# A banded attention and feed-forward kernel: its list scheduler models the SBUF port pair, one integer step works on halfwords, and the matrix engine is given unread products

## The chip, the cores and the metric

The kernel runs on one core of a Trainium2 chip. The metric is device time in microseconds of one execution. The engines are named as in the profile: PE (matrix engine), PEld (its weight loads), DVE (vector), ACT (scalar), POOL (GpSimd) and SP (the queue that issues most transfers).

## The reference, cut to what matters

```python
scores = scale * np.matmul(q, k.transpose(0, 1, 3, 2))        # q, k, v: 4 x 8 heads x 768 x 64
keep = is_global | is_local                                    # first 8 columns, or the last 96
scores = np.where(keep, scores - slopes * dist, -1000000000.0)
a = softmax(scores)
x = matmul(a, v)            # then laid out as 4 x 768 x 512
xn = (x - mu) / np.sqrt(var + 1e-06) * g_ln
ch = np.maximum(xn @ w_ch1, 0.0) @ w_ch2                       # 512 -> 2048 -> 512, float64 weights
out = x + ch
```

## The kernel before, in words

The 3072 rows are 24 tiles of 128. A tile *t* goes through attention over two blocks of keys (its own and the one before it; the first tile of each of the four batches has one block and is called short). Two tiles make a chunk *c* for the feed-forward part. The four short tiles come first (t = 0 to 3, chunks 0 and 1) and are computed in float32 straight from the loaded data; the other tiles use pairs of float16 numbers, a high part and a low part, and so do all feed-forward products (three products for each one wanted).

Before the feed-forward part can start, the float64 weights have to become such pairs. `weight(n)` (line 279) does it for 16 pieces, 8 of the first matrix and 8 of the second. A piece is loaded (`wb`), and then goes through six passes of 1024 elements per partition: `below` (`wr`, ACT), `signs` (`ws`, DVE, copies the sign bit into the low word), `sizes` (`wz`, ACT), `whole` (`ww`, DVE), `upper` (`wu`, the high part: POOL for the pieces in LIGHT, else ACT) and `lower` (`wl`, the low part by a subtraction, POOL).

The names of the other steps, which are also keys of the plan: for a short tile `tk`, `tq` are transpositions of keys and queries on PE, `km`, `qm` the copies out of PSUM. For group *g* of a tile: `S` scores (PE), `R` mask and minimum (DVE), `E` exponentials (ACT), then for short tiles a transposition `tp` (PE) and its copy `pl`; for the other tiles `ph` (the high part, DVE), `pl` (the low part, POOL) and `pt` (a transposing transfer); `P` is the product with the values (PE, tile `pv`). Then `X` divides, `B`, `A`, `W`, `C` normalize (`W` is a power of 128 x 1 numbers on POOL), `xr`, `xt`, `xh`, `xl` transpose the result into `xT`. `F{c}_{f}` is a step of the first feed-forward product (24 matmuls, 256 columns wide, needs both tiles' `xl` and pieces 2j and 2j+1 of the weights, j = f // 4), followed by `hh` (ACT) and `hl` (DVE); `G` is a step of the second product.

The order on every engine is not that of the code: `class Plan` (line 78) takes all steps as tasks with an engine, a cost, predecessors, a rank and buffer tokens, runs a list scheduler over them with those costs, and the instructions of each engine are written in the order that comes out. Nothing is reordered on the chip afterwards, so a task whose input is late holds up what is queued behind it on its engine. Each PSUM and SBUF buffer pool is a token count in `plan.room`. Before, the plan takes an engine as given for each task, and each engine as independent of the others:

```python
LIGHT = (0, 1, 2, 3, 4, 5, 9, 11, 13, 14)
task(f"ws{n}", "DVE", 1.22, signs, [f"wr{n}"], rank=rank)
task(f"ww{n}", "DVE", 1.22, whole, [f"wz{n}"], rank=rank)
task(f"wl{n}", "POOL", 2.4, lower, [f"wu{n}"], rank=rank)
```

All instructions that the plan writes carry line 169 in the profile (the body of `made` in `Lane`), so rows are told apart by their tiles: `w2h`, `w2l`, `st` are the places where weight pieces are worked on, `f` the PSUM tile of a feed-forward step, `r` the reciprocal of the exponentials' sum at the start of `X`.

## Time and profile before

| | us |
|---|---|
| median of 3 runs (645.90 to 646.12) | 646.03 |
| the profiled execution | 646.06 |
| its span, first to last instruction | 644.30 |
| outside the span | 1.76 |
| PE busy | 608.2 |
| DVE busy | 398.3 |
| ACT busy | 277.3 |
| POOL busy | 218.2 |

[...] A start-to-start distance of two neighbours in an engine's timeline is what an instruction costs in a full queue; its duration is a little longer, since neighbours overlap.

### The profile page before, as it was taken

To read this page: it belongs to the slowest core of one execution; us is meant where nothing else is said; L and a number is where in the kernel's file an instruction comes from. 1 tells how busy PE (TensorE), PEld (TensorE's weight loads), DVE (VectorE), ACT (ScalarE), POOL (GpSimd) and SP (SyncE) were. 2 spreads that over 40 slices of the span, in tenths; PEclk is the share of its full clock that TensorE was granted. 3 is DMA by queue.
4 is the path that set the end of the run, shared out by engine and by line. 5 is a ranking of instruction groups with operands and counts; after the bars stand their busy time and mean duration, and the time that the engine had idled before them with its cause. 6 is when DMAs were issued, how large, how long until landed. Compare 5 with 4: busy or idle time off the path is not lost.

```text
span 644.3 us, 13414 instructions
## 1 busy us (share of the span) xinstructions
PE 608.2 (94%) x5266; PEld 436.3 (68%) x5266; DVE 398.3 (62%) x953; ACT 277.3 (43%) x729; POOL 218.2 (34%) x172
## 2 busy tenths in 40 slices
PE   5678699799999999999999999999999999999995
PEld 4567488455885885885885875875875875874852
DVE  4799999896575565546555646555645645546740
ACT  3877477554363353344443343443443433330200
POOL 4476667574243223223223222322323222120000
PEclk9857799999999999999999999999999999999999
DMA  8941777968996665688577585686686664241000
GB/s 240 308 187 66 213 180 201 244 130 164 221 162 137 153 132 108 139 159 156 129 146 139 114 160 113 152 172 115 143 144 117 121 125 82 51 66 34 17 4 35
DMA packets 247303, 88.26 MB, mean 137 GB/s; under 512 B 237376, under 2 KB 237376, under 8 KB 247232
## 3 DMA queue, kind: packets, MB, share of 16 engines
q1 hardware_dynamic: 246944, 87.32, 62.0%
q8 instruction: 43, 0.70, 0.5%
q14 instruction: 28, 0.23, 0.1%
q10 hardware_dynamic: 288, 0.00, 0.0%
HBM read 38.01 MB, written 6.29 MB: 69 GB/s over the span
## 4 chain that ended last, share of the span: by engine, by line
PE 83%; DVE 9%; ACT 3%; issue 2%; DMA 1%; POOL 1%; ACTq 0%; DVEq 0%; POOLq 0%
PE f L169 71%; PE s L169 6%; PE pv L169 5%; DVE st L169 3%; DVE w2h L169 1%; ACT T L169 1%; DVE h L169 1%; DMA nn<-in_n_local_dram 1%; DVE w2l L169 1%; ACT w2h L169 1%; DVE T L169 1%; DMA pT<-pn 0%; DVE qn L169 0%; POOL w1l L169 0%; ACT st L169 0%
## 5 line engine op out<-in xcount | busy, mean ns | idle before, releaser
L169 PE MATMUL f<-xT,w1h 128*128 128x256 f16 x1536 | 260.6, 276 | 8.3 <-DVE h L169 8.3
L169 PE MATMUL f<-w2h,h 128*128 128x512 f16 x768 | 238.2, 379 | 3.7 <-DVE h L169 3.7
L169 PE MATMUL f<-xT,w1l 128*128 128x256 f16 x768 | 212.2, 276 | 0.1
L169 PEld LDWEIGHTS <-h 128*128 128x128 f16 x1152 | 109.7, 98 | 126.2 <-issue 2.3
L169 POOL TENSOR_TENSOR pn<-T,pn 128x512 f16<-128x512 f32 x80 | 95.4, 1193 | 232.9 <-DVE pn L169 121.4
L169 PEld LDWEIGHTS <-w1h 128*128 128x128 f16 x1536 | 150.3, 99 | 27.4 <-DVE h L169 6.0
L169 PE MATMUL f<-w2l,h 128*128 128x512 f16 x384 | 145.5, 379 | 0.0
L169 ACT ACTIVATE h<-f 128x512 f16<-128x512 f32 x96 | 56.7, 591 | 93.1 <-PE f L169 92.8
L169 ACT ACTIVATE T<-T,mn 128x256 f32<-128x256 f32 (+1 forms) x192 | 92.4, 482 | 4.3 <-ACT mn L169 0.4
L169 DVE SCALAR_TENSOR_TENSOR h<-f,h 128x512 f16<-128x512 f32 x96 | 65.5, 686 | 31.2 <-ACT h L169 30.7
L169 PEld LDWEIGHTS <-w1l 128*128 128x128 f16 x768 | 76.2, 99 | 10.1 <-POOL w1l L169 0.4
L169 DVE CAST pn<-T 128x512 f16<-128x512 f32 x80 | 38.2, 479 | 67.7 <-ACT T L169 66.0
L169 DVE CUSTOM_DVE_ANT_0 T<-s,mask 128x256 f32<-128x256 f32 (+1 forms) x192 | 68.0, 395 | 13.4 <-PE s L169 13.1
L169 ACT ACTIVATE mn<-nm 128x2 f32<-128x2 f32 (+1 forms) x88 | 17.6, 200 | 136.2 <-DVE nm L169 136.1
L169 PE MATMUL s<-kT,qT 128*128 128x128 f16 (+1 forms) x704 | 58.9, 233 | 2.8 <-DVE d L169 2.8
L169 PEld LDWEIGHTS <-pT 128*128 128x128 f16 x960 | 38.9, 98 | 12.4 <-DMA pT<-pn 0.6
L169 POOL TENSOR_TENSOR kn<-kf,kn 128x512 f16<-128x512 f32 x24 | 29.0, 1209 | 45.6 <-ACT kn L169 36.4
L169 DVE SCALAR_TENSOR_TENSOR x<-f,x 128x512 f32<-128x512 f32 x24 | 16.2, 687 | 45.6 <-PE f L169 45.6
L169 PE MATMUL pv<-vn,pT 128*128 128x64 f16 x960 | 41.0, 193 | 0.1
L169 PEld LDWEIGHTS <-qT 128*128 128x128 f16 x640 | 38.5, 98 | 2.4
L169 POOL TENSOR_TENSOR rs<-rs,half 128x1 f32<-128x1 f32 x24 | 23.6, 983 | 48.9 <-DVE rs L169 47.8
L169 ACT ACTIVATION_READ_ACCUMULATOR T<-T,mn 128x1 f32 x192 | 35.8, 186 | 0.0
(114 smaller groups left out, 498.6 us busy)
## 6 DMA issues: line engine op xcount, KB each, us to landing
st<-in_moe_w_ch_dram SPq DMA_DIRECT2D x10, 1024.0 KB, 5.8
kf<-in_k_dram SPq DMA_DIRECT2D x28, 256.0 KB, 3.9
vf<-in_v_dram SPq DMA_DIRECT2D x28, 256.0 KB, 3.4
qf<-in_q_dram SPq DMA_DIRECT2D x24, 256.0 KB, 4.0
out_dram<-x SPq DMA_DIRECT2D x24, 256.0 KB, 2.5
qT<-qT SPq DMA_DIRECT2D x40, 128.0 KB, 2.5
w2h<-in_moe_w_ch_dram SPq DMA_DIRECT2D x3, 1024.0 KB, 8.7
w2l<-in_moe_w_ch_dram SPq DMA_DIRECT2D x3, 1024.0 KB, 7.0
```

The source lines that it names most:

```text
L169: ins = getattr(self.engine, name)(*args, **kw)
```

## The change

- The plan knows that DVE and POOL exclude each other: a task with `port=True` on DVE, and every task on POOL, starts no earlier than the last such task ended (`port` in `order`).
- A task may name several engines with a cost on each. The plan then takes the engine on which it would end first, with ACT favoured by 1.1 us and POOL burdened by 1.1 us (`SIDE`). This holds for both mask tables, the copies out of PSUM, the high and low parts of keys, values, queries and probabilities, `wu`, `wl`, `xr` and `hh`. LIGHT is gone.
- `signs` writes the top halfword of the low word from the top halfword of the high word (one source, 16 bits), where it combined two 32-bit operands.
- `blank` is a product of the identity with itself, 512 columns wide, into a PSUM bank that nobody reads. Where the plan sees PE idle before time 90, it writes as many of them as fit the gap at 0.22 us each.
- The bank for them is taken from `pv`, which has one bank left where it had two.
- The numbers that set ranks (QUICK, PIECE, START) and many costs are new.

```diff
-QUICK = (0.0, 2.2, 22.1, 36.5)
-PIECE = (20.2, 5.8, 11.5)
-START = 43.0
-LIGHT = (0, 1, 2, 3, 4, 5, 9, 11, 13, 14)
+QUICK = (0.0, -5.2, 7.7, 16.9)
+PIECE = (1.8, 5.3, 15.0)
+START = 37.6
+SIDE = (-1.1, 1.1)
+UNTIL = 90.0
...
+FAVOR = {"ACT": SIDE[0], "POOL": SIDE[1]}
+EITHER = {"ACT": 0.62, "DVE": 0.7}
+BLANK = 0.22
...
+                    costs = tasks[key][0]
+                    if len(costs) > 1:
+                        ends = {o: max(ready[o][key], engines[o]) + c + FAVOR.get(o, 0.0) for o, c in costs.items()}
+                        if ends[engine] > min(ends.values()):
+                            continue
...
+                    if engine == "POOL" or (tasks[key][8] and engine == "DVE"):
+                        t = max(t, port)
...
+            if engine == "PE" and self.blank and t < self.until:
+                order += [(t, len(order), self.blank)] * int((t - engines[engine] - 0.1) / (BLANK if t > 6.0 else 2.0 * BLANK))
+            if engine == "POOL" or (shared and engine == "DVE"):
+                port = t + cost
...
-    ps_v = ctx.enter_context(tc.tile_pool(name="ps_v", bufs=2, space=PSUM))
+    ps_v = ctx.enter_context(tc.tile_pool(name="ps_v", bufs=1, space=PSUM))
...
+    def blank():
+        if "blank" not in made:
+            made["blank"] = ps_v.tile([P, 2, 2 * P], F32, tag="blank", name="blank")
+        words = ident.bitcast(F16)
+        pe.matmul(made["blank"], lhsT=words[:, :P], rhs=words.unsqueeze(1).to_broadcast([P, 2, 2 * P]), start=True, stop=True)
...
         def signs():
-            lo, hi, _, _ = staged[n]
-            vec.scalar_tensor_tensor(out=lo, in0=hi, scalar=SIGN, in1=lo, op0=ALU.bitwise_and, op1=ALU.bitwise_or)
+            vec.tensor_scalar(out=halves[n][:, :, 1], in0=halves[n][:, :, 3], scalar1=0x8000, scalar2=None, op0=ALU.bitwise_and)
...
-        def lower():
-            pool.tensor_tensor(out=dl, in0=staged[n][3], in1=dh, op=ALU.subtract)
+        def lower(engine):
+            (pool if engine == "POOL" else vec).tensor_tensor(out=dl, in0=staged[n][3], in1=dh, op=ALU.subtract)
...
-        task(f"ws{n}", "DVE", 1.22, signs, [f"wr{n}"], rank=rank)
+        task(f"ws{n}", "DVE", 0.7, signs, [f"wr{n}"], rank=rank, port=True)
...
+        task(f"wu{n}", {"ACT": 1.17, "POOL": 1.95, "DVE": 0.75}, 0, upper, [f"ww{n}"] + (["wl1"] if n == 8 else []) + (["wl3"] if n in (8, 9, 10, 11) else []) + (["wl7", "wl8"] if n >= 12 else []), rank=rank, port=True)
+        task(f"wl{n}", {"POOL": 2.2, "DVE": 1.24}, 0, lower, [f"wu{n}"], rank=rank, port=True)
...
-                task(f"ph{t}_{g}", "DVE", 0.44, lambda g=g: high(g), [f"E{t}_{g}"], rank=rank - 3, take={"pn": [f"pt{t}_{g}"]})
-                task(f"pl{t}_{g}", "POOL", 1.2, lambda g=g: low(g), [f"ph{t}_{g}"], rank=rank - 3)
+                task(f"ph{t}_{g}", {"ACT": 0.64, "DVE": 0.45}, 0, lambda engine, g=g: high(g, engine), [f"E{t}_{g}"], rank=rank - 3, take={"pn": [f"pt{t}_{g}"]}, port=True)
+                task(f"pl{t}_{g}", {"POOL": 1.22, "DVE": 0.7}, 0, lambda engine, g=g: low(g, engine), [f"ph{t}_{g}"], rank=rank - 3, port=True)
```

In the whole program, of the 80 low parts of probabilities (`pl`) 79 go from POOL to DVE, all 80 high parts (`ph`) from DVE to ACT, 15 of the 16 `wl` from POOL to DVE, and PE has 71 blanks beside its 5092 other matmuls.

What stands on PE around its first feed-forward step `f1_0_0`. Before, the last work of tile 2 and the scores of tile 3 (`s3`) stand ahead of it:

```order
L169 MATMUL pv2_446<-vf1_0_271,pT2_0_424 128x64 x4
L169 MATMUL tp2_1_457<-ident_89,T2_1_419 128x128 x4
L169 MATMUL s3_0_468<-kT00_0_455,qT3_451 128x128 x4
L169 MATMUL s3_1_476<-kT00_0_455,qT3_451 128x128 x4
L169 MATMUL pv2_446<-vf1_0_271,pT2_1_473 128x64 x4
L169 LDWEIGHTS w1h_83
L169 MATMUL f1_0_0_495<-xT0_259,w1h_83 128x256
```

Now, with a blank between:

```order
L193 MATMUL tp2_0_480<-ident_89,T2_0_432 128x128 x4
L193 MATMUL tk3_493<-ident_89,kf0_0_402 128x128 x4
L193 LDWEIGHTS ident_89
L193 MATMUL blank_118<-ident_89 128x512
L193 LDWEIGHTS w1h_83
L193 MATMUL f1_0_0_500<-xT0_331,w1h_83 128x256
```

The second half of tile 2 and all scores of tile 3 now come after `f1_0_0`, spread between the steps of chunk 0.

What POOL has from the mask table to the weight pieces (`rs` is `W`). Before:

```order
L169 TENSOR_SCALAR mask_88<-d 128x256 x8
L169 TENSOR_TENSOR rs<-rs,half 128x1
L169 TENSOR_TENSOR w1h<-w2h,fill 128x2x512
L169 TENSOR_TENSOR w1l<-w2h,w1h 128x2x512
L169 TENSOR_TENSOR w1h<-w2h,fill 128x2x512
L169 TENSOR_TENSOR w1l<-w2h,w1h 128x2x512
L169 TENSOR_TENSOR rs<-rs,half 128x1
L169 TENSOR_TENSOR w1h<-w2l,fill 128x2x512
L169 TENSOR_TENSOR w1l<-w2l,w1h 128x2x512
```

Now, up to the last instruction that POOL has for the first weight matrix:

```order
L193 TENSOR_SCALAR mask_88<-d 128x256 x2
L193 TENSOR_TENSOR rs<-rs,half 128x1 x2
L193 TENSOR_TENSOR w1h<-w2l,fill 128x2x512
L193 TENSOR_TENSOR rs<-rs,half 128x1
L193 TENSOR_TENSOR w1l<-st_463,w1h 128x2x512
L193 TENSOR_TENSOR rs<-rs,half 128x1
```

POOL keeps one `upper` (piece 2) and one `lower` (piece 6) of the first matrix; the other passes went to DVE and ACT.

What DVE has around the low parts of `xT`, which the first feed-forward step waits for. Before, at tile 0's:

```order
L169 SCALAR_TENSOR_TENSOR w2h<-w2h 128x1024 x2
L169 TENSOR_TENSOR xT_259<-tx_299,xT_259 128x4x128
L169 TENSOR_SCALAR qT_334<-tq_321 128x512
L169 SCALAR_TENSOR_TENSOR w2h<-w2h 128x1024
L169 COPY pT_360<-tp_339 128x512
```

Now:

```order
L193 TENSOR_TENSOR xT_331<-tx_458,xT_331 128x4x128
L193 TENSOR_TENSOR xT_331<-tx_447,xT_331 128x4x128
L193 CAST w1h<-w2l 128x2x512
L193 TENSOR_TENSOR w1l<-w2l,w1h 128x2x512 x2
L193 TENSOR_SCALAR st_353<-st_353 128x1024
L193 TENSOR_SCALAR st_380<-st_380 128x1024
L193 SCALAR_TENSOR_TENSOR h_0_554<-f_0_0_500,h_0_554 128x512
```

Both tiles' parts of `xT` stand together; then come the casts and subtractions of pieces 2 and 3, two sign steps as one-source halfword instructions, and the low part of the first feed-forward step.

## Rows read from the trace of the kernel before

**Rows 1.** Busy time by stretches, cut at the first step of chunk 0, at the first step of chunk 1 and at the last product of the second matrix: the stretch and its length, then us busy (x instructions) of PE, PEld, DVE, ACT and POOL, then the granted clock, the DMA share and GB/s.
```profile
0.00:49.85 49.85, 33.26 (x177) 28.23 (x177) 36.41 (x111) 32.20 (x85) 25.66 (x27) 0.81 0.76 238
49.85:89.44 39.59, 31.24 (x225) 25.21 (x226) 37.77 (x50) 25.31 (x51) 25.70 (x13) 0.80 0.51 148
...
160.00:610.00 450.00, 450.00 (x4149) 324.28 (x4147) 253.85 (x675) 175.40 (x494) 120.34 (x106) 1.00 0.63 126
...
636.83:644.30 7.47, 0.11 (x2) 0.00 (x0) 1.10 (x5) 0.00 (x0) 0.00 (x0) 0.86 0.14 46
```

**Rows 2.** What PE waited for (us in total, times, longest us): the largest of the whole span, and the only one from 100 us on.
```profile
PE f L169 <- DVE h L169: 12.0, 5, 4.7
...
PE f L169 <- DVE h L169: 3.7, 2, 2.0
```

**Rows 3.** PE in order of time: start, length, then the operation and how many are merged. Scores (four heads a group, two groups here), the first feed-forward step, its second triple, a transposition beside feed-forward triples at a later time, and the first step of chunk 1.
```profile
19.43 1.71 PE L169 MATMUL s<-kT,qT 64*128 64x128 f32 x16
...
49.85 0.63 PE L169 MATMUL f<-xT,w1h 128*128 128x256 f16 x2
...
50.49 0.63 PE L169 MATMUL f<-xT,w1h 128*128 128x256 f16 x2
...
57.64 0.60 PE L169 MATMUL tp<-ident,T 128*128 128x128 f32 x4
58.08 0.38 PE L169 MATMUL f<-xT,w1h 128*128 128x256 f16 x2
...
58.40 0.38 PE L169 MATMUL f<-xT,w1h 128*128 128x256 f16 x2
...
89.44 0.38 PE L169 MATMUL f<-xT,w1h 128*128 128x256 f16 x2
```

**Rows 4.** The same view by stretches of 4 us: float32 work on PE (first row), and the first feed-forward steps (second row).
```profile
44.00:48.00 4.00, 4.00 (x21) 3.51 (x20) 4.00 (x4) 3.06 (x6) 3.92 (x2) 0.50 0.00 0
...
52.00:56.00 4.00, 4.00 (x24) 3.03 (x23) 2.98 (x14) 0.81 (x3) 2.37 (x2) 0.62 0.12 44
```

**Rows 5.** DVE in order of time: the first mask table, four heads of `R` and what follows them, weight passes, the start and the end of `X` to `C`, and a cast of 512 elements.
```profile
8.33 1.17 DVE L169 TENSOR_SCALAR mask<-d 128x128 bf16<-128x128 f32 x8
...
40.11 0.28 DVE L169 CUSTOM_DVE_ANT_0 T<-s,mask 128x128 f32<-128x128 f32 x1
...
40.95 2.35 DVE L169 SCALAR_TENSOR_TENSOR w2l<-w2l 128x1024 int32<-128x1024 int32 x2
...
61.58 3.16 DVE L169 SCALAR_TENSOR_TENSOR w2h<-w2h 128x1024 int32<-128x1024 int32 x1
...
65.27 1.21 DVE L169 SCALAR_TENSOR_TENSOR st<-st 128x1024 int32<-128x1024 int32 x1
66.40 0.68 DVE L169 TENSOR_TENSOR xT<-tx,xT 128x512 f16<-128x512 f32 x1
67.00 0.67 DVE L169 COPY pT<-tp 128x512 f32<-128x512 f32 x1
...
72.53 2.11 DVE L169 TENSOR_SCALAR r<-sm 128x8 f32<-128x8 f32 x1
74.68 0.20 DVE L169 RECIPROCAL r<-r 128x8 f32<-128x8 f32 x1
...
77.46 0.68 DVE L169 SCALAR_TENSOR_TENSOR h<-f,h 128x512 f16<-128x512 f32 x1
...
121.08 0.41 DVE L169 CAST pn<-T 128x512 f16<-128x512 f32 x1
```

**Rows 6.** POOL in order of time, the subtractions and the power beside the DVE rows above.
```profile
39.61 0.99 POOL L169 TENSOR_TENSOR rs<-rs,half 128x1 f32<-128x1 f32 x1 [2.27 <-DVE rs L169]
...
60.66 3.00 POOL L169 TENSOR_TENSOR w1l<-st,w1h 128x1024 f16<-128x1024 f32 x1
...
66.56 1.90 POOL L169 TENSOR_TENSOR w1h<-st,fill 128x1024 f16<-128x1024 f32 x1 [2.89 <-DVE st L169]
68.53 6.09 POOL L169 TENSOR_TENSOR w1l<-st,w1h 128x1024 f16<-128x1024 f32 x2
```

**Rows 7.** Groups of instructions by line and tile: count, busy us, mean ns of one, idle time before them and what ended it; the sign and whole steps of the pieces worked on in `st`.
```profile
L169 DVE SCALAR_TENSOR_TENSOR st<-st 128x1024 int32<-128x1024 int32 x20 | 33.5, 1689 | 3.1 <-ACT st L169 3.1
```

**Rows 8.** ACT in order of time: the first exponentials' bias, the scaling of `xs`, one group of `E` from its bias to the next instruction, a copy out of PSUM, and a weight pass.
```profile
13.30 0.21 ACT L169 ACTIVATE mn<-nm 128x4 f32<-128x4 f32 x1 [5.75 <-DVE nm L169]
...
23.69 0.72 ACT L169 ACTIVATE xs<-xs,rs 128x512 f32<-128x512 f32 x1 [1.02 <-POOL rs L169]
24.32 0.19 ACT L169 ACTIVATE mn<-nm 128x4 f32<-128x4 f32 x1
...
26.10 0.57 ACT L169 ACTIVATE xT<-tx 128x512 f16<-128x512 f32 x1
26.57 0.19 ACT L169 ACTIVATE mn<-nm 128x4 f32<-128x4 f32 x1
...
28.83 1.15 ACT L169 ACTIVATE w2h<-w2h 128x1024 f32<-128x1024 f32 x1
```

**Rows 9.** A tile in the middle: its last product with the values and the next tile's first one on PE (start, length), and `x` of the division that reads the bank on DVE.
```profile
315.18 0.51 PE L169 MATMUL pv<-vn,pT 128*128 128x64 f16 x12
...
321.21 0.51 PE L169 MATMUL pv<-vn,pT 128*128 128x64 f16 x12
...
316.49 0.69 DVE L169 TENSOR_TENSOR x<-pv,r 128x512 f32<-128x512 f32 x1
```

More of the change, by code (lines that the diff above doesn't have):

```diff
@@ L75, in counted, with task @@
     return cnt
+FAVOR = {"ACT": SIDE[0], "POOL": SIDE[1]}
+EITHER = {"ACT": 0.62, "DVE": 0.7}
+BLANK = 0.22
 class Plan:
     def __init__(self, lag=0.12):
-        self.tasks, self.room, self.lag = {}, {}, lag
-    def task(self, key, engine, cost, fn, after=(), rank=0.0, take=None, dma=0.0, slack=0.0):
+        self.tasks, self.room, self.lag, self.blank, self.until = {}, {}, lag, None, 0.0
+    def task(self, key, engine, cost, fn, after=(), rank=0.0, take=None, dma=0.0, slack=0.0, port=False):
         assert key not in self.tasks, key
-        self.tasks[key] = [engine, cost, fn, [a for a in after if a is not None], rank, take or {}, dma, slack]
+        costs = dict(engine) if isinstance(engine, dict) else {engine: cost}
+        self.tasks[key] = costs, fn, [a for a in after if a is not None], rank, take or {}, dma, slack, isinstance(engine, dict), port
     def order(self):
         tasks, lag = self.tasks, self.lag
-        users, left = {}, {}
-        for key, (_, _, _, after, _, _, _, _) in tasks.items():
+        users, left, frees, holds = {}, {}, {}, {}
+        for key, (_, _, after, _, take, _, _, _, _) in tasks.items():
             left[key] = len(after)
@@ L102, in order, with open_ @@
-        ready = {}
-        at = {}
+        engines = {engine: 0.75 for task in tasks.values() for engine in task[0]}
+        ready = {engine: {} for engine in engines}
+        at, order, self.times, self.on = {}, [], {}, {}
+        def open_(key):
+            after, slack = tasks[key][2], tasks[key][6]
+            for engine in tasks[key][0]:
+                ready[engine][key] = max([self.times[a][1] + (lag if self.on[a] != engine else 0.0) for a in after], default=0.0) + slack
         for key in tasks:
@@ L105, in order @@
             if not left[key]:
-                ready.setdefault(tasks[key][0], {})[key] = 0.0
-        done, order, self.times = {}, [], {}
-        queue = 0.0
-        while any(ready.values()):
+                open_(key)
+        engines["PE"] = 1.5
+        queue, port = 0.0, 0.0
+        while len(self.times) < len(tasks):
             best = None
             for engine, able in ready.items():
-                now = engines.get(engine, 0.0)
-                start = {}
+                begin = {}
@@ L391, in both @@
             bank = "f1" if name == "k" and t < 3 else "f2"
-            task(f"t{name}{t}", "PE", 1.05, flip, [f"L{name}{t}", "ident"], rank=rank, take={bank: [f"{name}m{t}"]}, slack=0.5 * (t > 1))
-            task(f"{name}m{t}", engine, 0.66, move, [f"t{name}{t}"], rank=rank, take={"h" if name == "q" or own else "kT0": [f"S{t}_1"]})
-        both("k", lambda: home("kT0"), 1.0, "ACT")
-        both("q", lambda: hpool.tile([P, 4, P], F32, tag="h", name=f"qT{t}"), -QS, "DVE")
+            task(f"t{name}{t}", "PE", 0.7, flip, [f"L{name}{t}", "ident"], rank=rank, take={bank: [f"{name}m{t}"]}, slack=0.5 * (t > 1))
+            task(f"{name}m{t}", EITHER, 0, move, [f"t{name}{t}"], rank=rank, take={"h" if name == "q" or own else "kT0": [f"S{t}_1"]})
+        both("k", lambda: home("kT0"), 1.0)
+        both("q", lambda: hpool.tile([P, 4, P], F32, tag="h", name=f"qT{t}"), -QS)
     def keys(t, b, i, rank):
@@ L421, in keys @@
         task(f"Lk{name}", "SP", 0.57, lambda: fetch(raw, key, k, "k", b, i), rank=rank - 9, take={"ld": [f"kl{name}"]}, dma=1.47, after=[f"S{t - 2}_0"] if t > 5 else [f"wb{9}"])
-        task(f"kh{name}", "ACT", 0.62, high, [f"Lk{name}"], rank=rank, take={"ld": [f"kt{name}"]})
-        task(f"kl{name}", "POOL", 1.2, low, [f"kh{name}"], rank=rank)
+        task(f"kh{name}", {"ACT": 0.64, "DVE": 0.5}, 0, high, [f"Lk{name}"], rank=rank, take={"ld": [f"kt{name}"]}, port=True)
+        task(f"kl{name}", {"POOL": 1.22, "DVE": 0.7}, 0, low, [f"kh{name}"], rank=rank, port=True)
         task(f"kt{name}", "SP", 1.35, flip, [f"kl{name}"], rank=rank - 4, take={tag: last}, dma=1.47)
@@ L721, in ffn1 @@
         task(key, "PE", 2.62, products, after, rank=rank, take={tag: [f"hl{c}_{f}"]})
-        task(f"hh{c}_{f}", "ACT", 0.62, high, [key], rank=rank - 6, take={"h": last[c:c + 1] if c < 2 else last})
+        task(f"hh{c}_{f}", {"ACT": 0.62, "DVE": 0.72}, 0, high, [key], rank=rank - 6, take={"h": last[c:c + 1] if c < 2 else last})
         task(f"hl{c}_{f}", "DVE", 0.7, low, [f"hh{c}_{f}"], rank=rank - 6)
```

159 lines of the change are left out of this document (85 added, 74 removed).

## The prediction

> **What bounds the kernel now.** I read the stretches first. From 160 us to 610 us PE is busy in every microsecond at clock 1.00, so nothing that only frees DVE, ACT or POOL there can move the end [rows 1]. What can be won lies ahead of 160 us. Up to the first step of chunk 0, at 49.85 us, PE worked 33.26 us at a mean clock of 0.81; from there to the first step of chunk 1, at 89.44 us, it worked 31.24 of 39.59 us at 0.80 [rows 1, 3]. PE's waits say whom it waited for: the largest is 12.0 us for the low parts `h` on DVE, of which only 3.7 us lie behind 100 us [rows 2]. DVE was busy 37.77 of the 39.59 us, so DVE bounds that stretch [rows 1].
>
> The next view is DVE in order of time beside POOL. A weight pass with two operands costs 1.13 us where POOL is quiet (from 65.27 to 66.40), and 3.16 us at 61.58, where it ends 1.08 us after POOL's subtraction ended at 63.66 [rows 5, 6]. The tiny `r` (8 elements) took 2.11 us at 72.53, ending as POOL's pair of subtractions, 68.53 to 74.62, ends [rows 5, 6]. So a DVE instruction beside a POOL instruction waits for its end, and the 20 passes in `st` took 1.69 us each instead of 1.13 [rows 7]. Both engines count as busy while one stands still.
>
> The last view is the clock. It read 0.50 from 44 to 48 us, with PE busy in all 4 us on float32 work, and rose inside 52 to 56, some 5 us after the feed-forward steps began [rows 4]. At half clock a triple of their matmuls takes 0.64 us (49.85 to 50.49), at full clock 0.32 (58.08 to 58.40) [rows 3].
>
> **The frame of the sum.** The matmuls behind the first step of chunk 1 are the same in number before and after. From 89.44 to the last product at 636.83 are 547.4 us, then 7.5 us to the end of the span [rows 1], and 1.76 us lie outside the span: 646.06 us for the profiled execution, which is the median within 0.1 us. So the forecast is the new time of the first step of chunk 1, plus 556.7.
>
> **Up to the first step of chunk 0.** Half of the first mask table (8 on DVE, 1.17 us from 8.33) goes to ACT, and the scores no longer wait for it, only `R` does. `R` can start between 9.6 us (masks done) and 11 us (scores run at half clock); I take 10.2, the nearer to the masks' row. Four heads of `R` cost 0.84 us (40.11 to 40.95) [rows 5], so the first exponentials start at 11.2 us, against 13.30 before [rows 8]. From there the new order keeps ACT in work. Ahead of the high parts of both `xT` it has five groups of exponentials at 1.78 us (24.32 to 26.10), eight copies at 0.47, eight weight passes at 1.15 and two scalings at 0.63 [rows 8]: 8.9 + 3.8 + 9.2 + 1.3 = 23.2 us. That gives 34.4, and one low part on DVE, 0.60 us (66.40 to 67.00) [rows 5], gives 35.0 as the floor. To it I add two waits. ACT waits for tile 1's `R`, which stands on DVE behind the mask table that shares the port with POOL: between 0 and 2 us, I take 1.2. And `ww3` on DVE falls beside POOL's `wu2`, 1.90 us when alone [rows 6], of which I take 1.1. **The first step starts at 37.3 us**, 12.6 us earlier. Tile 2's second half and tile 3's scores are no longer ahead of it, but they are not gone: they count below.
>
> **From there to the first step of chunk 1.** PE has eight steps of 24 matmuls at 0.107 (20.8 us), six sets of transpositions at 0.44 (57.64 to 58.08), two groups of scores at 0.86 (1.71 for two), four groups of products with values that I price like scores, and 14 blanks, whose 512 columns cost two feed-forward matmuls, 0.21 us [rows 3]. That is 20.8 + 2.6 + 1.7 + 3.4 + 2.9 = 31.4 us. DVE has in the same stretch nine passes or subtractions of 1024 elements at 1.13, six sign steps, eleven instructions at 0.60, three splits at 0.68, two `R` at 0.84 and two chains from `X` to `C` at 3.0 (2.78 from 74.68 to 77.46, and `r`) [rows 5]. The sign step is not in the trace. The nearest row is a cast with one source, 512 elements in 0.41 us [rows 5]; twice the elements give about 0.6 to 0.7, and the bound on the other side is 1.13, no gain at all. I take 0.60. The sum is 10.2 + 3.6 + 6.6 + 2.0 + 1.7 + 6.0 = 30.1 us. So PE and DVE are almost level, and PE's sum is the floor. On top of it comes what POOL still does on the shared port while DVE is full: two `W` at 0.99 and one `lower`, priced by the nearest row, 1.90 [rows 6]: 3.9 us. **The first step of chunk 1 starts at 37.3 + 31.4 + 3.9 = 72.6 us**, 16.8 us earlier than 89.44.
>
> [...]
>
> **Behind it.** The low parts of the probabilities, 79 subtractions of 512 elements, move from POOL to DVE, and the casts ahead of them from DVE to ACT. DVE had 253.85 of 450 us of work, ACT 175.40 [rows 1]. 79 at about 0.68, less the casts at 0.41, add some 20 us to DVE; 80 copies at about 0.6 add some 48 us to ACT. Both stay far below 450, so PE hides it and I cost it at nothing; if that cover were gone, each microsecond late on PE counts in full. The single `pv` bank: a tile's last product starts at 315.18, the division that empties the bank ends at 317.18, and the next tile's first product starts at 321.21 [rows 9]. That leaves 4.0 us, so it costs nothing either, and to eat the gain over 19 tiles the division would have to come 4.9 us later each time. The waits of 3.7 us behind 100 us [rows 2] may stay or go: 0 to -3.7; I keep them, since chunk 1's last low part is still needed for the second product. The sum is 72.6 + 556.7 = **629.3 us**.
>
> **Rivals.** (1) *The clock stays low and the blanks stand in the way*: the one that ends slower. Between the first scores and the first step, PE's own work is 6 groups of scores, 12 sets of transpositions, 4 of products and 42 blanks: 5.2 + 5.3 + 3.4 + 8.8 = 22.7 us at full clock, just what ACT needs. At half clock it is 45.4, PE becomes the bound, the first step starts at 9.6 + 45.4 = 55.0, its first 5 us run at half pace (+2.5), and the time is 649.5. It decides from a first step behind 54. For it: float32 work alone left the clock at 0.50 from 44 to 48 us though PE never paused [rows 4]. Against it: 8.8 of these 22.7 us are blanks, float16 products like the steps that raised the clock, and there are few pauses left. [...] (2) *The queues fall out of step*: a task that comes late holds all behind it. The old plan set START to 43.0 and the step came at 49.85, 6.85 us late; with START 37.6 and the same lateness it comes at 44.5, and the time is 636.5. For it: the orders are still frozen from costs. Against it: the lateness had a cause, the port, which the new order avoids. (3) *The halfword step is no cheaper*, so that part does not do what it says: 0.53 us more on ten sign steps, 5.3 us, 634.6. (4) *The bank makes PE wait* for the division: 19 us for each microsecond beyond the slack; nothing in rows 9 speaks for it.
>
> **How the numbers follow.** Forecast 0.66, rival (2) 0.20, (3) 0.07, (1) 0.05, (4) 0.02. The low end takes both floors and no waits behind 100 us: 35.0 + 31.4 + 556.7 - 3.7 = 619.4. The high end takes rival (2) and half of (3), 639. Range 620 to 639. A measurement here can tell about 0.2%, 1.3 us, from no change. All cases but (1) and (4) are far on the fast side: faster 0.93, within 0.02, slower 0.05.
>
> **What would show it.** First exponentials near 11 us; first step of chunk 0 near 37 and of chunk 1 near 73; DVE passes of 1024 elements near 1.13 us with few near 3; the sign step near 0.6; PE's clock at 1.00 from about 15 us on; no new PE wait behind 160 us. I am wrong if the clock still reads 0.50 at 30 us, if PE waits for `x` ahead of `pv`, or if the first step comes behind 45 us.

## The result, and the profile after

| | before | after |
|---|---|---|
| median, us | 646.08 (4 runs, 645.9 to 646.23) | 628.95 (4 runs, 625.83 to 629.47) |
| ratio, 95% interval | | 0.9725 [0.9693, 0.9757] |
| the profiled execution | 646.06 | 629.0 |
| its span | 644.30 | 627.1 |
| first step of chunk 0 / of chunk 1 | 49.85 / 89.44 | 40.18 / 76.05 |
| last product of the second matrix begins | 636.44 | 619.49 |

The forecast was 629.3. The total agrees within 0.4 us, but by luck: two of its terms were off by about the same amount in opposite directions, as the stretches show. (Busy time by stretches of the kernel after, cut at its first step of chunk 0, at that of chunk 1, and behind its last product; columns as in [rows 1], the granted clock being a share of the full one. First line: the profile's busy times, shares of the span and instructions.)

```profile
PE 611.4 (97%) x5337; PEld 434.5 (69%) x5337; DVE 404.2 (64%) x979; ACT 329.7 (53%) x823; POOL 51.5 (8%) x52
...
0.00:40.18 40.18, 33.92 (x194) 23.20 (x194) 31.23 (x103) 31.33 (x89) 10.23 (x15) 0.92 0.92 273
40.18:76.05 35.87, 33.99 (x279) 28.28 (x280) 33.17 (x60) 30.04 (x58) 3.93 (x3) 0.95 0.69 184
160.00:600.00 440.00, 440.00 (x4040) 316.87 (x4038) 260.53 (x656) 206.35 (x544) 26.15 (x27) 1.00 0.60 120
619.80:627.10 7.30, 0.19 (x3) 0.08 (x2) 1.09 (x5) 0.00 (x0) 0.00 (x0) 0.79 0.13 46
```

Against [rows 1]: the middle is PE-bound as before, and the tail is as long as before. The start is shorter, and PE now fills 34 of the 36 us between the two first steps, where it filled 31 of 40. The waits of PE say the same. (PE's waits after: us in total, times, longest. Above the last dots the whole span, below them all that is left from 76 us on.)

```profile
PE f L193 <- ACT kT L193: 2.2, 1, 2.2
PE f L193 <- DVE h L193: 1.6, 3, 1.0
...
PE f L193 <- DVE xT L193: 0.3, 1, 0.3
...
PE f L193 <- DVE h L193: 0.3, 1, 0.3
```

The 12.0 us for `h` of [rows 2] are 1.6 now. The 3.7 us behind 100 us, which the forecast kept, are 0.3. That is the first error. The second shows on DVE in order of time, with POOL in the block below it.

```profile
18.46 1.22 DVE L193 SCALAR_TENSOR_TENSOR w2h<-w2h 128x1024 int32<-128x1024 int32 x1
...
20.20 0.69 DVE L193 CAST w1h<-w2h 128x1024 f16<-128x1024 f32 x1
...
24.95 1.36 DVE L193 TENSOR_SCALAR w2h<-w2h 128x1024 uint16<-128x1024 uint16 x1
26.07 1.46 DVE L193 TENSOR_SCALAR w2l<-w2l 128x1024 uint16<-128x1024 uint16 x1
...
30.77 1.33 DVE L193 TENSOR_SCALAR w2l<-w2l 128x1024 uint16<-128x1024 uint16 x1
...
37.16 2.36 DVE L193 SCALAR_TENSOR_TENSOR w2l<-w2l 128x1024 int32<-128x1024 int32 x1
39.44 1.27 DVE L193 TENSOR_TENSOR xT<-tx,xT 128x512 f16<-128x512 f32 x2
```

```profile
25.18 2.40 POOL L193 TENSOR_TENSOR rs<-rs,half 128x1 f32<-128x1 f32 x1 [11.00 <-DVE rs L193]
...
36.52 1.92 POOL L193 TENSOR_TENSOR w1h<-w2l,fill 128x1024 f16<-128x1024 f32 x1 [4.38 <-issue]
49.60 0.92 POOL L193 TENSOR_TENSOR rs<-rs,half 128x1 f32<-128x1 f32 x1 [11.16 <-DVE rs L193]
64.26 2.46 POOL L193 TENSOR_TENSOR w1l<-st,w1h 128x1024 f16<-128x1024 f32 x1 [13.74 <-ACT w1h L193]
67.01 0.55 POOL L193 TENSOR_TENSOR rs<-rs,half 128x1 f32<-128x1 f32 x1 [0.29 <-DVE rs L193]
```

Three things are to be seen. The halfword sign step (`uint16`) takes 1.33 us, or 1.11 from start to start (24.95 to 26.07, 30.77 to 31.88), about what the two-source pass at 18.46 takes (1.22). That is not the 0.60 of the forecast; the cast of the same 1024 elements, at 0.69, comes near it. The long rows of [rows 5] are nearly gone: what is left is `ww3` at 37.16, which ends 1.1 us after POOL's `wu2` (36.52 + 1.92 = 38.44), as forecast. And the exclusion works in the other direction too: POOL's power of 128 x 1 numbers takes 0.92 us at 49.60, which is also the median of its 24, but 2.40 at 25.18, where it ends with the second of two sign steps on DVE (26.07 + 1.46 = 27.53).

The chain of ACT, which the forecast summed up for the first step, has waits that the sum didn't have. (ACT in order of time after; in brackets the idle time ahead and what ended it.)

```profile
10.67 1.24 ACT L193 ACTIVATE w2h<-w2h,less 128x1024 int32<-128x1024 uint32 x1 [1.41 <-DMA w2h<-in_moe_w_ch_dram]
11.81 0.20 ACT L193 ACTIVATE mn<-nm 128x4 f32<-128x4 f32 x1
...
21.60 0.60 ACT L193 ACTIVATE pT<-tp 128x512 f32<-128x512 f32 x1 [0.51 <-PE tp L193]
...
23.80 0.60 ACT L193 ACTIVATE pT<-tp 128x512 f32<-128x512 f32 x1 [0.49 <-PE tp L193]
...
30.90 1.16 ACT L193 ACTIVATE w1h<-w2h 128x1024 f16<-128x1024 f32 x1 [1.01 <-DVE w2h L193]
...
36.39 1.05 ACT L193 ACTIVATE xT<-tx 128x512 f16<-128x512 f32 x2
```

The first exponentials start at 11.81 (11.2 forecast), behind a weight pass that waited for its load. Two copies wait for transpositions on PE, 1.0 us together, and one weight pass 1.0 us for DVE. The high parts of both `xT` are done at 36.39 + 1.05 = 37.44. PE stands still for 2.16 us ahead of the first step, and up to chunk 1 it waits little more. (PE in order of time: the first step of chunk 0 and its second matmul, the two waits for `h`, and the first step of chunk 1.)

```profile
40.18 0.28 PE L193 MATMUL f<-xT,w1h 128*128 128x256 f16 x1 [2.16 <-ACT kT L193]
40.77 0.37 PE L193 MATMUL f<-xT,w1h 128*128 128x256 f16 x1 [0.31 <-DVE xT L193]
...
59.54 0.38 PE L193 MATMUL f<-xT,w1h 128*128 128x256 f16 x2 [0.96 <-DVE h L193]
...
63.54 0.38 PE L193 MATMUL f<-xT,w1h 128*128 128x256 f16 x2 [0.38 <-DVE h L193]
...
76.05 0.67 PE L193 MATMUL f<-xT,w1h 128*128 128x256 f16 x2
```

The two transpositions that ACT waits for fall into a stretch of low clock, and the wait ahead of the first step is followed by another. (The stretches of 4 us.)

```profile
16.00:20.00 4.00, 4.00 (x25) 3.58 (x23) 3.41 (x18) 3.94 (x16) 0.00 (x0) 0.57 1.01 412
20.00:24.00 4.00, 4.00 (x20) 3.51 (x19) 3.16 (x7) 3.00 (x9) 0.00 (x0) 0.58 0.97 268
36.00:40.00 4.00, 2.02 (x14) 1.20 (x11) 4.00 (x11) 3.97 (x17) 1.92 (x1) 1.00 0.97 314
40.00:44.00 4.00, 3.51 (x18) 2.38 (x19) 4.00 (x6) 2.43 (x3) 0.00 (x0) 0.57 0.67 248
```

### The profile page after: what moved, and what is told of

It is laid out like the page before. It is cut to its first block, busy times and chain, and to the rows that moved or that the text cites. A ratio compares the mean times of both kernels' runs of the same rounds, so it can differ in the third digit from the quotient of the medians.

```text
span 627.1 us, 13530 instructions
## 1 busy us (share of the span) xinstructions
PE 611.4 (97%) x5337; PEld 434.5 (69%) x5337; DVE 404.2 (64%) x979; ACT 329.7 (53%) x823; POOL 51.5 (8%) x52
## 4 chain that ended last, share of the span: by engine, by line
PE 89%; DVE 6%; DMA 1%; issue 1%; ACT 1%; SPq 0%; DVEq 0%; ACTq 0%
PE f L193 77%; PE s L193 6%; PE pv L193 5%; DVE st L193 1%; DVE w2l L193 1%; DMA w2h<-in_moe_w_ch_dram 1%; DVE T L193 1%; DVE h L193 1%; SPq L193 0%; ACT T L193 0%; DVE w2h L193 0%; DVE xT L193 0%; PE tp L193 0%; PE blank L193 0%; DVE x L193 0%
## 5 line engine op out<-in xcount | busy, mean ns | idle before, releaser
L193 PE MATMUL f<-xT,w1h 128*128 128x256 f16 x1536 | 256.5, 273 | 3.9 <-ACT kT L193 2.2
L193 PEld LDWEIGHTS <-w1h 128*128 128x128 f16 x1536 | 148.2, 98 | 21.6 <-DVE xT L193 2.5
L193 DVE TENSOR_TENSOR pn<-T,pn 128x512 f16<-128x512 f32 x79 | 56.0, 709 | 74.6 <-ACT pn L193 74.6
L193 POOL TENSOR_TENSOR rs<-rs,half 128x1 f32<-128x1 f32 x24 | 24.9, 1038 | 429.2 <-DVE rs L193 405.2
L193 PE MATMUL s<-kT,qT 128*128 128x128 f16 (+1 forms) x704 | 55.4, 226 | 1.2 <-ACT T L193 1.2
L193 ACT ACTIVATE pn<-T 128x512 f16<-128x512 f32 x80 | 50.1, 626 | 1.6
L193 PEld LDWEIGHTS <-pT 128*128 128x128 f16 x960 | 38.8, 98 | 10.3
L193 DVE TENSOR_TENSOR x<-pv,r 128x512 f32<-128x512 f32 x24 | 16.6, 691 | 9.5 <-PE pv L193 8.6
```

The source lines that it names most:

```text
L193: ins = getattr(self.engine, name)(*args, **kw)
```

## The experiments

Each kernel was run 4 to 12 times, in turn with the kernel before. The ratio is to the kernel before of the same job (646.08 us for the change, then 645.9, 646.67 and 646.85), and the last three columns come from one profiled execution each: the first step of chunk 0, the first product with the second matrix, and the start of the last one. Kernels are compared by their ratios.

| | median, us | ratio [95%] | chunk 0 | second matrix | last |
|---|---|---|---|---|---|
| before | 646.08 | 1 | 49.85 | 114.07 | 636.44 |
| after | 628.95 | 0.9725 [0.9693, 0.9757] | 40.18 | 99.78 | 619.49 |
| no_blanks | 631.7 | 0.9776 [0.9759, 0.9793] | 39.42 | 99.19 | 620.21 |
| word_sign | 629.62 | 0.9745 [0.9733, 0.9758] | 38.80 | 100.19 | 619.92 |
| zero_sign | 626.62 | 0.9716 [0.9693, 0.9739] | 38.79 | 96.92 | 616.66 |
| one_bank | 646.33 | 1.0009 [1.0001, 1.0018] | 49.78 | 113.54 | 636.00 |
| port_unseen | 628.35 | 0.9719 [0.9707, 0.9732] | 37.05 | 98.19 | 619.20 |
| blanks_before | 644.89 | 0.9983 [0.9969, 0.9997] | 49.59 | 113.51 | 635.84 |
| pool_low | 629.31 | 0.9745 [0.9727, 0.9764] | 38.63 | 98.11 | 618.98 |
| pool_weights | 639.71 | 0.9890 [0.9874, 0.9906] | 40.37 | 106.30 | 630.15 |
| lower_before | 646.42 | 0.9993 [0.9984, 1.0002] | 47.62 | 115.29 | 637.09 |
| half_sign | 624.84 | 0.9669 [0.9652, 0.9687] | 36.87 | 95.56 | 614.83 |
| true_cost | 629.5 | 0.9731 [0.9714, 0.9749] | 38.52 | 99.47 | 620.20 |
| pool_empty | 627.72 | 0.9707 [0.9692, 0.9722] | 34.00 | 95.22 | 616.81 |

**The unread products taken out.**

```diff
-    plan.blank, plan.until = blank, UNTIL
+    plan.blank, plan.until = None, UNTIL
```

> The changed kernel (628.95 us) without its 71 unread products; plan, order and all else as in it. Theory A: the start-up is won by the order and the engines, and the products only hold the clock up; without them the transpositions and scores ahead of the first step of chunk 0 run at half clock in part (0.9 us a set instead of 0.44, and about four sets lie in ACT's chain, +1.8) and the first 5 us of feed-forward steps run at half pace (+2.5): 632 to 634, clock 0.50 around 35 us. Rival B: in this order float32 work has so few pauses that the clock stays at 1.00 anyway, 629 +- 1. Rival C: the products stand in the way of late work and cost more than the clock gives, 626 to 628.

631.7 us, 0.005 of the time (3 us) more than after, about the size that theory A gave; the two intervals are only just apart. Its place is not shown: the profiled execution was the fastest of the five (629.52; the others 629.92 to 632.85). In it the clock is much lower ahead of 36 us, and the first step still comes no later than in the profiled execution after. (The stretches 0 to 36 and 36 to 60 us without the products, and then the same of the kernel after.)

```profile
0.00:36.00 36.00, 26.82 (x132) 23.66 (x133) 27.50 (x97) 27.96 (x76) 8.37 (x15) 0.74 0.90 268
36.00:60.00 24.00, 18.70 (x144) 15.73 (x143) 21.88 (x47) 20.53 (x51) 2.60 (x2) 0.86 0.51 179
```

```profile
0.00:36.00 36.00, 31.90 (x181) 21.99 (x182) 27.05 (x92) 27.18 (x73) 8.31 (x14) 0.91 0.91 268
36.00:60.00 24.00, 20.33 (x158) 16.23 (x156) 22.07 (x49) 20.79 (x55) 2.84 (x2) 0.93 0.49 173
```

So the clock is higher with the products in these two executions (0.91 for 0.74, 0.93 for 0.86; over the span of every run it is 0.989 to 0.998 with them and 0.976 to 0.994 without), but ACT and DVE bound the time ahead of the first step, and PE at a mean clock of 0.74 nearly keeps up with them there: ACT waits for it 1.0 us in all, as after. Rival C, that the products cost more than the clock gives, falls. In one place they do stand in the way: after, in the low stretch from 16 us on, two of them run at 19.65, and the transposition that ACT waits for starts only behind them, at 20.50.

**The old sign step in the new order.**

```diff
-            vec.tensor_scalar(out=halves[n][:, :, 1], in0=halves[n][:, :, 3], scalar1=0x8000, scalar2=None, op0=ALU.bitwise_and)
+            lo, hi, _, _ = staged[n]
+            vec.scalar_tensor_tensor(out=lo, in0=hi, scalar=SIGN, in1=lo, op0=ALU.bitwise_and, op1=ALU.bitwise_or)
```

> The changed kernel with the sign step of before (two 32-bit sources, 1.13 us from start to start) in the place of the halfword step, plan and order as in the changed kernel. The halfword step took 1.33 us there and 1.11 from start to start. Theory A: it is no cheaper, so nothing changes: 629 +- 1.3. Rival B: it does pay, if only where POOL works beside it, up to 0.5 us a step on ten steps: 632 to 634.

629.62 us, inside the interval of after: that part of the change is worth nothing that can be measured. (Groups by line and tile: count, busy us, mean ns of one, idle; first of the kernel after, then with the old step, where both passes are in one group.)

```profile
L193 DVE SCALAR_TENSOR_TENSOR st<-st 128x1024 int32<-128x1024 int32 x10 | 13.2, 1317 | 0.0
L193 DVE TENSOR_SCALAR st<-st 128x1024 uint16<-128x1024 uint16 x10 | 13.1, 1329 | 0.0
```

```profile
L193 DVE SCALAR_TENSOR_TENSOR st<-st 128x1024 int32<-128x1024 int32 x20 | 25.1, 1267 | 0.0
```

**The sign as a product with zero.**

```diff
-            vec.tensor_scalar(out=halves[n][:, :, 1], in0=halves[n][:, :, 3], scalar1=0x8000, scalar2=None, op0=ALU.bitwise_and)
+            vec.tensor_scalar(out=halves[n][:, :, 1].bitcast(BF16), in0=halves[n][:, :, 3].bitcast(BF16), scalar1=0.0, scalar2=None, op0=ALU.mult)
```

> The changed kernel with the sign step as a multiplication by 0.0 of the same halfwords read as bfloat16, written to the same place (a signed zero is the sign bit). Theory A: the integer operation is what makes the halfword step take 1.33 us; a float one on the same strides takes 0.60 to 0.70, as the cast of the same 1024 elements does (0.69). Then the term of my sum holds: first step of chunk 0 about 1 us earlier (two of four steps on the way of ACT and DVE), six steps of 0.5 us less behind it, at most 4 us in all: 625 to 627, first step of chunk 1 at 72 to 74. Rival B: the stride of 8 bytes on 16-bit words sets the pace, the step stays at 1.3 and the time at 629 +- 1.3. Rival C: the step gets cheaper and nothing is won because PE is the floor behind 40 us: 628 to 629.

```profile
L193 DVE TENSOR_SCALAR st<-st 128x1024 bf16<-128x1024 bf16 x10 | 13.2, 1340 | 0.0
```

The step takes 1.34 us, as rival B had it: the integer operation isn't what makes it slow. Of what differs from the cast at 0.69, 16-bit reads with a stride of 8 bytes, writes with one, or reading and writing the same tile, this doesn't say which. The median, 626.62, lies in the range of theory A, but not for its reason, since the step got no cheaper; and the five runs (625.72 to 630.2) lie across the four of after (625.83 to 629.47), so no gain is shown. Work and order are the same in both kernels; what differs between their profiled executions is the clock (0.99 from 36 to 60 us here, 0.93 after), and the second matrix starts earlier here (96.92 for 99.78).

**One bank for p x v, in the kernel before.**

```diff
-    ps_v = ctx.enter_context(tc.tile_pool(name="ps_v", bufs=2, space=PSUM))
+    ps_v = ctx.enter_context(tc.tile_pool(name="ps_v", bufs=1, space=PSUM))
...
-pv=2
+pv=1
```

> The kernel before (646.1 us) with one bank for p x v in the place of two, nothing else. Theory A: 4.0 us of slack in the middle, so it costs nothing: 646 +- 1.3, no PE wait for x. Rival B: with POOL contention the division comes late in some of the 19 tiles: 1 us each on a part of them, 650 or more, with a PE wait ahead of pv.

646.33 us, 0.1% more: the bank costs nothing that matters, as the slack in [rows 9] said.

**A plan that doesn't see the port.**

```diff
-                        t = max(t, port)
+                        t = max(t, 0.0)
```

> The changed kernel with a plan that doesn't see the shared port (the line that holds a start back is void); choice among engines, burden of 1.1 us on POOL, costs, ranks and products as in the changed kernel, so the order comes out a little different. Theory A: what won the start-up is that POOL was emptied, and the choice with its burden does that without the port rule; the order differs little: 629 +- 2. Rival B: the order under the port rule is what keeps DVE from standing still; without it passes of 2 to 3 us come back on DVE ahead of 76 us, each 1 to 2 us: 633 to 638.

628.35 us: theory A. With POOL burdened in the choice of an engine, little is left on it ahead of 100 us (15.0 us busy), and the rule has hardly anything to order. The first step of chunk 0 even comes at 37.05 here, and the last product only 0.3 us before that of after. Beside the burden on POOL, the part that gives the change its name is worth nothing that can be measured; the rule without the burden was not tried.

**Unread products in the kernel before.** One bank for p x v, `blank` as in the change, and in the old `order`:

```diff
+            if engine == "PE" and self.blank and t < 90.0:
+                order += [(t, self.blank)] * int((t - engines.get(engine, 0.0) - 0.1) / (0.22 if t > 6.0 else 0.44))
```

> The kernel before with one bank for p x v and unread products in the gaps that its own plan sees on PE before time 90 (34 or so), nothing else. Theory A: the clock is worth no more here than in the changed kernel, where taking the products out cost 2.8 us: the first feed-forward steps at full clock (-2.5) and little else, because DVE bounds what follows: 643 to 646. Rival B: the low clock (0.50 from 35 to 55 us) is a large part of the late start, so the first step comes 5 us or more earlier: 636 to 641. Rival C: the plan's gaps lie elsewhere than the real ones, the products hold up late work: 647 to 650.

644.89 us, 0.2% less, in the range of theory A; the first step comes at 49.59 for 49.85. The trace has 40 products, 35 of them ahead of the first step. The last six of these run from 34.84 to 37.58, so none stands in the 12 us ahead of the first step, and the clock is as low there as in [rows 4]. (Stretches of this kernel.)

```profile
44.00:48.00 4.00, 4.00 (x21) 3.44 (x21) 4.00 (x4) 3.05 (x5) 3.84 (x2) 0.50 0.00 0
48.00:52.00 4.00, 4.00 (x21) 3.35 (x22) 3.86 (x12) 3.29 (x11) 2.84 (x2) 0.53 0.76 249
```

This says that the products bring little in that order, not what a full clock would bring.

**The low parts of the probabilities back on POOL.**

```diff
-{"ACT": 0.64, "DVE": 0.45}, 0, lambda engine, g=g: high(g, engine)
+{"DVE": 0.45}, 0, lambda engine, g=g: high(g, engine)
...
-{"POOL": 1.22, "DVE": 0.7}, 0, lambda engine, g=g: low(g, engine)
+{"POOL": 1.22}, 0, lambda engine, g=g: low(g, engine)
```

> The changed kernel with the low parts of the probabilities back on POOL and the high parts back on DVE (80 of each), the plan knowing it. Theory A: behind 160 us PE covers it, as DVE and ACT have room; what may come back is the wait for h behind 100 us, 3.7 us before and 0.3 in the changed kernel: 629 to 633. If it comes back, the emptied POOL is what removed it; if not, the low parts of the weights were. Rival B: the shared port slows DVE in the middle too and PE begins to wait there: more than 635.

629.31 us: the largest move of the change by count, 79 instructions to DVE and 80 to ACT, is worth nothing, as the forecast had it. The wait for `h` behind 100 us is 1.4 us here, for 0.3 after and 3.7 before, so these parts may account for a piece of it.

**The low parts of the weights back on POOL.**

```diff
-        task(f"wl{n}", {"POOL": 2.2, "DVE": 1.24}, 0, lower,
+        task(f"wl{n}", {"POOL": 2.2}, 0, lower,
```

> The changed kernel with all 16 low parts of the weights on POOL, as before, the plan knowing it and the port. Theory A: POOL's 1.9 to 3 us a piece exclude DVE, which needs 1.13 for the same: about six pieces fall ahead of the first step of chunk 1, 0.8 to 1.9 us each, +5 to +11 there, and the wait for h behind 100 us comes back, up to 3.7: 634 to 643. Rival B: DVE is full there, POOL takes work off it and the plan puts it where DVE has port-free work: 627 to 630.

639.71 us: 0.0165 of the time, 10.7 us, are given back, theory A. The first step comes at 40.37 as after (40.18); all is lost behind it, 6.5 us up to the second matrix and the rest behind. DVE's rows are long again, and the waits for `h` with them. (Groups of DVE, then PE's longest waits, of this kernel.)

```profile
L193 DVE TENSOR_SCALAR w2h<-w2h 128x1024 uint16<-128x1024 uint16 x3 | 5.9, 1981 | 0.0
L193 DVE SCALAR_TENSOR_TENSOR w2l<-w2l 128x1024 int32<-128x1024 int32 x3 | 5.0, 1679 | 0.0
```

```profile
PE f L193 <- DVE h L193: 5.6, 3, 2.6
```

From the first step to 160 us PE stands still for 7.3 us, for 2.3 after: 5.0 of the 10.7 us. Another 4.0 us are unread products. The plan sees the waits coming and writes 32 products behind the first step, where after has 14, and they keep PE busy for 7.72 us in the place of 3.67. The rest, some 1.6 us, may be the clock: it is 0.94 from 76 to 106 us and 0.97 from there to 160, where after has 1.00 (but 0.95 up to 76 us).

**The same move alone, in the kernel before.**

```diff
-        task(f"wl{n}", "POOL", 2.4, lower, [f"wu{n}"], rank=rank)
+        task(f"wl{n}", "DVE", 1.24, lower, [f"wu{n}"], rank=rank)
```

(with `vec` for `pool` in `lower`)

> The kernel before (646.1 us) with one change: the 16 low parts of the weights on DVE in the place of POOL, priced 1.24 in the plan; no port rule, no products, two banks, old ranks. Putting them back on POOL cost the changed kernel 10.8 us. Theory A: they are the main part wherever they stand, since DVE loses 1.9 to 3 us to each on POOL and needs 1.13 to do it itself: 635 to 640, wait for h behind 100 us near 0. Rival B: the gain needs the rest of the change (the high parts off POOL, the casts on ACT, the ranks); alone, DVE, which is the bound, only gets more work: 643 to 648.

646.42 us: rival B. The same move that is worth 10.7 us in the new order is worth nothing in the old one. The groups say why: the passes did get shorter, by as much as DVE took over. (DVE's groups up to 100 us, columns as above, of this kernel and then of the kernel before.)

```profile
L169 DVE SCALAR_TENSOR_TENSOR st<-st 128x1024 int32<-128x1024 int32 x11 | 17.3, 1612 | 0.0
L169 DVE SCALAR_TENSOR_TENSOR w2l<-w2l 128x1024 int32<-128x1024 int32 x6 | 8.6, 1438 | 0.0
L169 DVE SCALAR_TENSOR_TENSOR w2h<-w2h 128x1024 int32<-128x1024 int32 x6 | 8.3, 1402 | 1.0 <-ACT w2h L169 1.0
...
L169 DVE TENSOR_TENSOR w1l<-st,w1h 128x1024 f16<-128x1024 f32 x3 | 3.6, 1211 | 0.0
```

```profile
L169 DVE SCALAR_TENSOR_TENSOR st<-st 128x1024 int32<-128x1024 int32 x12 | 21.0, 1771 | 1.8 <-ACT st L169 1.8
L169 DVE SCALAR_TENSOR_TENSOR w2h<-w2h 128x1024 int32<-128x1024 int32 x6 | 12.1, 2024 | 2.6 <-ACT w2h L169 2.6
L169 DVE SCALAR_TENSOR_TENSOR w2l<-w2l 128x1024 int32<-128x1024 int32 x6 | 11.3, 1893 | 0.0
L169 DVE TENSOR_SCALAR r<-sm 128x8 f32<-128x8 f32 x4 | 5.6, 1411 | 0.0
```

The three groups of passes took 21.0 (12 passes), 12.1 and 11.3 us before, and the four `r` another 5.6. In this kernel it is 17.3 (11 passes), 8.3 and 8.6, and 0.6 for the `r`: 21.0 - 17.3 - 1.6 (the missing pass) + 3.8 + 2.7 + 5.0 = 13.6 us less for the same work. The eleven low parts that DVE now does up to there cost 11 x 1.21 = 13.3. DVE stays the bound: it is busy for 83.4 of the first 100 us, 83.3 before. High parts and masks still stand on POOL and hold it up (1.4 to 1.6 us a pass, not 1.2), and its copies and casts still stand on DVE.

**Half of the sign step.** The step is left out for the second half of the weights:

```diff
-out=halves[n][:, :, 1], in0=halves[n][:, :, 3]
+out=halves[n][:, :512, 1], in0=halves[n][:, :512, 3]
```

> The changed kernel with the halfword sign step on the first 512 of each 1024 weights alone, so the others lose their signs; order and all else as in the changed kernel. A step should take about 0.7 us in the place of 1.33, which is the price that my sum gave it (0.60). Theory A: that price was the missing part of the stretch between the two first steps: 0.5 us on six to ten steps, of which PE's own work takes back what it needs: first step of chunk 1 at 72 to 74 in the place of 76, 625 to 627.5. Rival B: PE is the floor there by then, and the lateness is in PE's clock and in waits on ACT: 628 to 629.5.

```profile
L193 DVE TENSOR_SCALAR st<-st 128x512 uint16<-128x512 uint16 x10 | 7.3, 749 | 0.0
...
36.87 0.28 PE L193 MATMUL f<-xT,w1h 128*128 128x256 f16 x1 [1.24 <-ACT pT L193]
```

At 0.75 us a step, near its price in the forecast, the first step of chunk 0 comes at 36.87 and that of chunk 1 at about 72.3 (forecast 37.3 and 72.6), and the time is 624.84 us, 0.0056 or 3.6 us less than after. So theory A holds in size, but not in place: from first step to first step it is some 35.4 us, after 35.87. The gain lies ahead of the first step. It isn't all the step's either: word_sign, zero_sign and pool_low, with a step of full length and a clock of 0.96 to 1.00 ahead of 36 us, have the first step at 38.6 to 38.8, and the profiled execution after, at 0.91, at 40.18. In those three ACT never waits for a transposition behind its first exponentials, where after it waits 1.0 us. Of the 3.3 us between 40.18 and 36.87 some 1.4 thus go with the low stretch and 1.9 with the step, an estimate from single executions. It is not the clock alone: no_blanks, at 0.74, has the first step at 39.42.

**The true price in the plan.** `ws` priced 1.12, QUICK (0, -8.91, 8.73, 22.15), PIECE (-1.65, 10.99, -29.11), START 53.14, SIDE (-1.32, 1.18).

```diff
-        task(f"ws{n}", "DVE", 0.7, signs, [f"wr{n}"], rank=rank, port=True)
+        task(f"ws{n}", "DVE", 1.12, signs, [f"wr{n}"], rank=rank, port=True)
```

> The changed kernel with the sign step priced at its measured 1.12 in the plan in the place of 0.7, and the ranks (QUICK, PIECE, START, SIDE) searched anew for the earliest end of the plan's own clock. Theory A: a wrong price of 0.42 on 16 steps put tasks in an order that waits; the plan's end should come 1 to 3 us earlier on the chip: 626 to 628. Rival B: the list is robust against it, DVE's sum is the same in any order: 629 +- 1.3. Rival C: the new order has waits that the plan doesn't see, 630 or more.

629.5 us: rival B. A price that is 0.4 us off, on 16 tasks, does no harm to the list that can be measured.

**And POOL emptied.** The price as above, no POOL in the choices for `mask1`, `wu` and `wl`, QUICK (0, -7.35, 8.97, 23.85), PIECE (2.12, 3.82, 5.37), START 30.5, SIDE (-1.23, 5.24).

```diff
-{"POOL": 0.87, "ACT": 0.42, "DVE": 0.3}
+{"ACT": 0.42, "DVE": 0.3}
...
-{"ACT": 1.17, "POOL": 1.95, "DVE": 0.75}
+{"ACT": 1.17, "DVE": 0.75}
...
-{"POOL": 2.2, "DVE": 1.24}
+{"DVE": 1.24}
```

> As true_cost (price 1.12, ranks searched anew), and POOL may take neither a mask nor a high or low part of the weights, so that only the powers and a few key parts stay on it. Theory A: each of the four or five pieces that POOL kept ahead of 76 us made a DVE instruction 1.1 to 1.2 us longer; without them the first steps come 1 to 2 us earlier each: 625 to 627. Rival B: DVE and ACT are full there and the work that POOL gives up costs them as much: 628 to 631.

627.72 us, between the two theories. It is the lowest ratio of the versions that compute everything, but its interval [0.9692, 0.9722] overlaps that of after, so it isn't shown to be faster than that. Against true_cost, from which it differs by POOL's part in the choices and by ranks searched anew, all its five runs (626.99 to 628.27) are faster than all of that kernel's (628.42 to 630.65). In the profiled execution the first step comes 6.2 us earlier than after, the second matrix 4.6 and the last product 2.7: more than half is given back on the way.

## Why the prediction was right

- **The bound and the place of the gain: right.** Of the 17.0 us by which the last product comes earlier, 14.3 are won up to the start of the second matrix. Most of the 2.7 behind it are PE's waits ahead of 160 us: from the start of the second matrix up to there it stands still for 2.05 us before and for 0.28 after. The middle and the tail are as before. (In the working, the 1.69 us of [rows 7] is a duration; it compares with the 1.21 that such a pass lasts alone [rows 5], not with the 1.13 from start to start.)
- **First exponentials at 11.2: nearly.** 11.81, the rest being a weight pass ahead of them that waited 1.41 us for its load. The masks' share in it was not tried by itself.
- **First step of chunk 0 at 37.3: 2.9 us too early.** By the rows, 0.6 of it is the later start. ACT's own work up to the high parts of `xT` is 23.6 us for 23.2 (+0.4). ACT's waits are 2.0 us for 1.2 (+0.8), and they are other ones: the wait for tile 1's `R` isn't in the trace, but 1.0 us for transpositions on PE in a low stretch is, and 1.0 us for a weight pass on DVE behind the sign steps. The last 1.0 us is `ww3`. It does end 1.1 us after POOL's `wu2`, but it also stands ahead of the low parts of `xT` on DVE, and so they start at 39.44, 2.0 us after ACT's high parts are done. Of these, the wait for transpositions is missing in three profiled executions with a higher clock, and the wait for DVE in half_sign, where the step came at 36.87.
- **The sign step at 0.60: the term that was mis-sized.** It took 1.33, or 1.11 from start to start, near the other bound. With 1.11 on six steps the forecast's sum for DVE between the first steps, 30.1, becomes 33.2, which is what DVE was busy there (33.17), and it no longer lies below the 31.4 of PE. 1.33 is the condition of rival (3), and word_sign confirms that this part of the change does nothing. Rival (3)'s price, 5.3 us, was too high: half_sign gives 3.6, part of it clock, and it falls ahead of the first step, not behind it where the sum had six of the ten.
- **From first step to first step 35.3: right in size, 35.87 measured,** but by other terms. PE was busy for 33.99 us where the sum gave it 31.4 (8 x 24 x 0.107 is 20.5, not the 20.8 that stands in it). 3.51 of them fell in a stretch at a clock of 0.57, so some 1.5 us of the surplus are clock (an estimate: 3.51 x 0.43). PE stood still for 1.9 us where I had put 3.9 for POOL, and not for POOL: 1.34 of it are waits for `h`, at 59.54 and 63.54, both over before POOL's `lower` starts at 64.26, and behind that PE doesn't wait at all up to chunk 1. So that term was nil. Ahead of the first step POOL did wait for one-source steps: its power of 2.40 us ends with a sign step. `port` is the plan's name for this; the traces show the waits, not what the two engines share.
- **The waits behind 100 us kept at 3.7: wrong by 3.4.** They went to 0.3. From the first step of chunk 1 to the start of the last product it is 543.4 us, 547.0 before. In pool_weights 2.1 us of them stand, in pool_low 1.4, and lower_before, with the low parts of the weights on DVE but those of the probabilities on POOL, has 1.4 too. So neither kind of instruction made them alone.
- **The sum: right by two errors.** 76.05 for 72.6 is 3.45 too late, the waits are 3.4 too many. half_sign removes the first error, and its time, 624.84, is near the 629.3 - 3.4 = 625.9 that the forecast would have had without the second.
- **Rival (1), the clock: wrong in its price.** The forecast looked for 1.00 from about 15 us on, and it was 0.57 and 0.58 from 16 to 24 us and 0.57 from 40 to 44. That the blanks would raise it was my estimate: two of them ran at 19.65, and in stretches of 0.5 us the clock read 0.50 from 17 to 23 us. But PE was for the most part not the bound ahead of the first step. **Rival (2): over a third of it**: the step came 2.6 us behind START, not 6.85. **Rival (4): no.**
- **What made the gain.** I argued from the port, and the runs correct that. The port rule in the plan is worth nothing beside the burden on POOL (port_unseen). The low parts of the weights on DVE are worth 10.7 us in the new order (pool_weights) and nothing in the old one (lower_before). In neither run were the ranks searched anew, so a part of both results may be ranks that fit the other engine. With the low parts on POOL the new order still has its first step at 40.37, and wins 0.011 of the time, 7 us. Taken out one at a time, the port rule, the products, the halfword step and these low parts all leave the first step of chunk 0 at 37 to 40.4, and the single bank alone did nothing in the kernel before. What is left is the choice of engines, the ranks and the costs, and with them the first step comes 9.5 us earlier. That taking the low parts from POOL pays only once other work has left DVE is argued from DVE's busy times, not tried step by step. Which of the masks, casts, copies and ranks brings the first step forward was not taken apart. The unread products add some 3 us, at a place that the profile of the fastest execution doesn't show.

## What to carry to other kernels

When two engines exclude each other, moving work from one to the other saves what the exclusion costs and adds what the work takes. Sum both on the engine that is the bound before counting a gain, and relieve that engine elsewhere in the same change. A price that no row shows should be measured at the access pattern in question, strides and all, since a cast of as many elements, at 0.69 us, was no guide to a strided 16-bit step at 1.33. A forecast that hits should still be checked term by term: here two errors of 3.4 us hid each other.
